# Chunks 8 and 9 transposed by the DMA crossbar, with shallower load buffers and a moved schedule, in a fused RetNet recurrence and gated FFN

## The chip, the cores and the metric

The kernel runs on one core of one Trainium2 chip. The metric is the device time of one execution in microseconds. Each run was repeated, and the times below are medians with all or the extreme runs beside them. In the profile, PE is TensorE, PEld its weight loads, DVE is VectorE, ACT is ScalarE, POOL is GpSimd and SP is SyncE. A "q" behind an engine's name (SPq) stands for its queue, from which DMAs are issued. "L183" is line 183 of the kernel that the profile belongs to. In the changed kernel the lines from L60 to about L530 carry a number one lower than in the kernel before.

With one core there is no other core to compare with, so a run is called slow when it is over 1.5% above the fastest run of the same kernel.

## The reference

The first part is a linear recurrence over 768 steps in 4 batches and 8 heads of width 64. Its output, as 3072 tokens of width 512, goes through a sigmoid-gated feed-forward of width 1536.

```python
state = gamma[None, :, None, None] * state + np.einsum('bhd,bhe->bhde', k[:, :, t], v[:, :, t])
y[:, :, t] = scale * np.einsum('bhd,bhde->bhe', q[:, :, t], state)
...
x = np.ascontiguousarray(attn_out.transpose(0, 2, 1, 3)).reshape(B * S, H * D)
gate = 1.0 / (1.0 + np.exp(-(x @ w_gate)))
val = x @ w_val
return (gate * val @ w_out).astype(np.float32)
```

## The kernel before

The recurrence is done in 24 chunks of 128 tokens, six for each batch. A chunk needs its k and q transposed. Then come the scores (k times q), masks on VectorE, the product of the masked scores with v, and the sum of k times v that is handed on as the state. The feed-forward runs over six blocks t of 512 tokens, that is four chunks each. The work of later chunks is put between the matmul groups of block t, according to a plan of (group number, step, chunks).

There are two ways to transpose. Chunks 4 to 9 use TensorE, with a copy by ScalarE behind it. Chunks 10 to 23 use the DMA crossbar, issued by SyncE. The loads are issued by GpSimd.

```python
ld = ctx.enter_context(tc.tile_pool(name="ld", bufs=10))
...
def load_v(g):
    vf[g] = ld.tile([C, H, D], F32, tag="vf", name="vf", bufs=8)
    nc.gpsimd.dma_start(out=vf[g], in_=src(v, g))

def load_kq(g):
    kn[g] = ld.tile([C, H, D], BF16, tag="kn", name="kn")      # 10 buffers
    qn[g] = ld.tile([C, H, D], BF16, tag="qn", name="qn")
    nc.gpsimd.dma_start(out=kn[g], in_=src(k, g))
    nc.gpsimd.dma_start(out=qn[g], in_=src(q, g))
...
def transposes(g):                                             # on TensorE
    tp = bank([128, 2 * NP, C], BF16)
    for i, x in enumerate((kn[g], qn[g])):
        for p in range(NP):
            nc.tensor.transpose(tp[:, i * NP + p, :], pair(x, p), ident)
    qkT[g] = at.tile([128, 2 * NP, C], BF16, tag="qkT", name="qkT", bufs=6)
    nc.scalar.activation(qkT[g], tp, AX.Copy)

def xbar(g):                                                   # by the DMA crossbar
    qkT[g] = ld.tile([128, 2 * NP, C], BF16, tag="qkX", name="qkX", bufs=8)
    for i, x in enumerate((kn[g], qn[g])):
        nc.sync.dma_start_transpose(out=qkT[g][:, i * NP:(i + 1) * NP, :],
                                    in_=x.rearrange("s h d -> s (h d)"))
...
def block(done, new):   # two chunks' outputs and the next two chunks' scores
    for g in olds: inter(g)
    for g in news: scores(g)
    for g in olds: intra(g)
    if news:
        zz[new] = pz.tile([128, 2, NP, D], F32, tag="z", name="z")
        for i, g in enumerate(news):
            if g % NCH < NCH - 1:      # a batch's last chunk hands no state on
                state(g, zz[new][:, i], True)
    ...                                # (cut: y_out, masks, state sums)
...
1: [(0, casts, 6), (1, step_t, 9), (3, block, 6, 8), (5, casts, 8), (7, scale_v, 10), ...
```

`step_t` is the TensorE transpose with the scaling of v; `scale_v` is that scaling alone. At t = 1 the first ups are split in halves of 256 columns, so that they can start on the first half of the tokens.

Of the kernel before, what the change touches and what calls it, by code (L numbers as in the profile page):

```python
# [9 lines left out]
F32 = mybir.dt.float32  # L10
# [7 lines left out]
def kernel(  # L18
# [11 lines left out]
    B, H, S, D = q.shape  # L30
    N_TOK, D_MODEL = out.shape
    D_FF = moe_w_gate.shape[1]
    C = 128
# [7 lines left out]
    ctx.enter_context(tc.manual_schedule())  # L41
    const = ctx.enter_context(tc.tile_pool(name="const", bufs=1))
    wpool = ctx.enter_context(tc.tile_pool(name="wpool", bufs=1))
    ld = ctx.enter_context(tc.tile_pool(name="ld", bufs=10))
    at = ctx.enter_context(tc.tile_pool(name="at", bufs=2))
    ffn = ctx.enter_context(tc.tile_pool(name="ffn", bufs=3))
    pz = ctx.enter_context(tc.tile_pool(name="pz", bufs=1, space=bass.MemoryType.PSUM))
# [2 lines left out]

    NG = B * NCH
    NT = N_TOK // 512
    XBAR = 10
    qn, kn, vf = {}, {}, {}

    def src(x, g):
        b, c = divmod(g, NCH)
        return x[b, :, c * C:(c + 1) * C, :].rearrange("h s d -> s h d")

    def load_v(g):  # L60
        vf[g] = ld.tile([C, H, D], F32, tag="vf", name="vf", bufs=8)
        nc.gpsimd.dma_start(out=vf[g], in_=src(v, g))  # L62

    def load_kq(g):
# [5 lines left out]
    def load_chunk(g):  # L70
        load_kq(g)
        load_v(g)
# [80 lines left out]
    def bank(shape, dt=F32):  # L153
        return pf.tile(shape, dt, tag="ff", name="ff")
# [12 lines left out]
    def xbar(g):  # L167
# [4 lines that stand above are left out]
# [68 lines left out]
    def x_cols(t, kk, lo, hi):  # L240
        if hi - lo == 512:
            return xT[t][:, :, kk, :]
        half = lo // 256
        return xT[t][:, half, kk, lo - half * 256:hi - half * 256]
# [132 lines left out]
    def up(t, n1, lo=0, hi=512):  # L377
        if t not in hT:
            hT[t] = ffn.tile([128, NFF, 512], BF16, tag="hT", name="hT", bufs=2)
        ps = []  # L380
        for w in (wg, wv):
            u = bank([128, 512])
            for kk in range(KT):
                nc.tensor.matmul(u[:, lo:hi], w[:, kk, n1 * 128:(n1 + 1) * 128], x_cols(t, kk, lo, hi),  # L384
                                 start=(kk == 0), stop=(kk == KT - 1))
            ps.append(u)
        gs = ffn.tile([128, 512], F32, tag="gs", name="gs")
        nc.scalar.activation(gs[:, lo:hi], ps[0][:, lo:hi], AX.Sigmoid)  # L388
        nc.vector.tensor_tensor(hT[t][:, n1, lo:hi], gs[:, lo:hi], ps[1][:, lo:hi], op=ALU.mult)  # L389

    def up_columns(t, n1s, lo, hi, rows=1):
        if t not in hT:
            hT[t] = ffn.tile([128, NFF, 512], BF16, tag="hT", name="hT", bufs=2)
        n = hi - lo
        us = [bank([128, 512]), bank([128, 512])]
        for row in range(rows):
            for w, u in zip((wg, wv), us):
                for i, n1 in enumerate(n1s):
                    for kk in range(row * KT // rows, (row + 1) * KT // rows):
                        nc.tensor.matmul(u[:, i * n:(i + 1) * n], w[:, kk, n1 * 128:(n1 + 1) * 128],  # L400
                                         x_cols(t, kk, lo, hi), start=(kk == 0 and (rows == 1 or i == 0)),
                                         stop=(kk == KT - 1), skip_group_check=rows > 1)
        ps = [u[:, :len(n1s) * n] for u in us]
        gs = ffn.tile([128, 512], F32, tag="gs", name="gs")
        g = gs[:, :len(n1s) * n]
        nc.scalar.activation(g, ps[0], AX.Sigmoid)  # L406
        nc.vector.tensor_tensor(hT[t][:, n1s[0]:n1s[-1] + 1, lo:hi], g.rearrange("p (i n) -> p i n", n=n),  # L407
                                ps[1].rearrange("p (i n) -> p i n", n=n), op=ALU.mult)
# [22 lines left out]
    def last_down(t):  # L431
        row = t * 512 + 384
        first = 0
        for i, width in enumerate((256, 128, 128)):
            o = bank([128, 512])
            for n1 in range(NFF):
                nc.tensor.matmul(o[:, :width], hT[t][:, n1, 384:512], wo[:, n1, first:first + width],  # L437
                                 start=(n1 == 0), stop=(n1 == NFF - 1))
            ob = ffn.tile([128, width], F32, tag=f"ob{width}", name="ob", bufs=2)
            if i == 1:  # L440
                nc.scalar.copy(ob, o[:, :width])
                nc.scalar.dma_start(out=out[row:row + 128, first:first + width], in_=ob)
            else:
                nc.vector.tensor_copy(ob, o[:, :width])
                nc.sync.dma_start(out=out[row:row + 128, first:first + width], in_=ob)
            first += width
# [78 lines left out]
    def ups(t):  # L525
        return [lambda n1=n1: up(t, n1) for n1 in range(NFF)]

    def downs(t):
        return [lambda sm=sm, i=i: down(t, sm, i) for sm in range(4) for i in range(2)]

    plan = {
        0: [(6, step_t, 4), (7, step_t, 5), (8, block, None, 4), (9, step_t, 6), (10, casts, 4), (10, step_t, 7),
            (12, block, 4, 6), (13, step_t, 8)],
        1: [(0, casts, 6), (1, step_t, 9), (3, block, 6, 8), (5, casts, 8), (7, scale_v, 10), (9, scale_v, 11),
            (11, block, 8, 10), (13, casts, 10), (14, scale_v, 12), (15, scale_v, 13), (18, block, 10, 12),
            (20, casts, 12)],
        2: [(0, scale_v, 14), (1, scale_v, 15), (4, block, 12, 14), (6, casts, 14), (11, scale_v, 16),
            (12, scale_v, 17), (16, block, 14, 16), (18, casts, 16)],
        3: [(3, scale_v, 18), (4, scale_v, 19), (6, block, 16, 18), (8, casts, 18), (12, scale_v, 20),
            (13, scale_v, 21), (15, block, 18, 20), (17, casts, 20)],  # L540
        4: [(3, scale_v, 22), (4, scale_v, 23), (6, block, 20, 22), (8, casts, 22), (14, block, 22, None)],
        5: [],
    }
    for t in range(NT):
        groups = ups(t) + downs(t)
        if t == NT - 1:
            groups[-2:] = [lambda: last_down(t)]
        if t == 0:
            groups = groups[6:]
            for g in range(8, 12):  # L550
                load_chunk(g)
        if t == 1:
            groups[:6] = [lambda n1=n1: up(1, n1, 0, 256) for n1 in range(6)]
            groups[6:6] = [lambda n1=n1: up_columns(1, range(n1, n1 + 2), 256, 512) for n1 in range(0, 6, 2)]
            for g in range(12, 16):
                load_chunk(g)
        if t == 2:
            load_chunk(18)
            load_chunk(19)
        if t == 3:  # L560
            load_chunk(22)
            load_chunk(23)
        for i, group in enumerate(groups):
            if t == 1 and i == 0:
                for g in range(XBAR, 12):
                    xbar(g)
            if i == len(groups) - 9:
                for g in range(4 * t + 8, 4 * t + 12):
                    if 12 <= g < NG:
                        xbar(g)  # L570
            if t == 1 and i == len(groups) - 4:
                load_chunk(16)
                load_chunk(17)
            if t == 2 and i == len(groups) - 4:
                load_chunk(20)
                load_chunk(21)
            group()
            for at_group, step, *g in plan[t]:
                if at_group == i:
                    step(*g)  # L580
# [30 lines left out]
```

## Time and profile before

| | before |
|---|---|
| median of 3 runs | 232.27 us (232.14 to 233.26) |
| span of the profiled run | 229.6 us |
| TensorE busy | 222.0 us, 97% of the span |
| DMA row full (9 tenths or more) | from the second to the 21st of 40 slices, to about 121 us; 7 tenths in the 22nd |
| granted clock | 1.00 |
| loads of k, q and v, median from issue to landing | 11.1, 12.4 and 10.5 us |

TensorE sets the end, so a microsecond saved or lost there is one in the time, as long as its inputs are there.

### The profile page before, as it was taken

Reading aid. Unit: us, or ns where it says so; the run is one execution under the profiler, and the core shown is the slowest. Engines: PE = TensorE matmul, PEld = TensorE weight load, DVE = VectorE, ACT = ScalarE, POOL = GpSimd, SP = SyncE. Lnnn points to the kernel's source line nnn. Section 1 sums busy time; section 2 is a strip of 40 time slices with the busy share of each in tenths; the row PEclk is TensorE's granted clock in tenths of the full one; section 3 lists DMA queues with packets and bytes.
Section 4 is the critical chain, followed back from the end, with each engine's and each line's share of the span. In section 5 each row is a group of like instructions: output and inputs, shape, how many; then the busy total and the mean of one; then the engine's idle time right before and its main releaser. Section 6 shows DMA issues by size and latency. Waiting matters only on the chain.

```text
span 229.6 us, 4530 instructions
## 1 busy us (share of the span) xinstructions
PE 222.0 (97%) x1834; PEld 120.9 (53%) x1834; DVE 119.1 (52%) x226; ACT 88.1 (38%) x161; POOL 75.3 (33%) x98
## 2 busy tenths in 40 slices
PE   4989999999999999999999999999999999999994
PEld 1558844558785455454445445445445454444444
DVE  5679444449875927458336267637267621243301
ACT  5964332465452423426321532612532512433221
POOL 7998666997843346723300000000000000000000
PEclk9999999999999999999999999999999999999999
DMA  7999999999999999999997342011100012100022
GB/s 140 179 228 197 198 206 207 235 241 246 178 155 108 158 147 175 251 123 135 121 177 190 104 91 46 0 50 64 74 3 0 0 49 91 46 0 3 0 91 93
DMA packets 75477, 27.56 MB, mean 120 GB/s; under 512 B 62016, under 2 KB 71104, under 8 KB 75456
## 3 DMA queue, kind: packets, MB, share of 16 engines
q0 software_dynamic: 55440, 16.78, 68.6%
q1 hardware_dynamic: 19872, 10.43, 24.5%
q8 instruction: 14, 0.23, 0.4%
q10 hardware_dynamic: 144, 0.07, 0.1%
q14 instruction: 7, 0.06, 0.1%
HBM read 28.31 MB, written 6.29 MB: 151 GB/s over the span
## 4 chain that ended last, share of the span: by engine, by line
PE 90%; POOL 3%; DMA 3%; ACT 1%; issue 1%; DVE 0%; POOLq 0%; ACTq 0%
PE ff L384 47%; PE ff L418 26%; PE ff L400 6%; DMA qr<-in_q_dram 3%; PE ff L233 2%; PE ff L184 2%; PE ff L196 2%; PE ff L163 1%; PE ff L437 1%; PE z L202 1%; POOL kr L77 1%; ACT gs L388 0%; POOL qr L77 0%; POOL vr L77 0%; POOL maskr L455 0%
## 5 line engine op out<-in xcount | busy, mean ns | idle before, releaser
L389 DVE TENSOR_TENSOR hT<-gs,ff 128x512 bf16<-128x512 f32 (+1 forms) x66 | 43.2, 662 | 58.9 <-PE ff L384 55.5
L384 PE MATMUL ff<-xT,wg 128*128 128x512 bf16 (+1 forms) x264 | 65.2, 369 | 0.0
L384 PE MATMUL ff<-xT,wv 128*128 128x512 bf16 (+1 forms) x264 | 65.2, 369 | 0.0
L388 ACT ACTIVATE gs<-ff 128x512 f32<-128x512 f32 (+1 forms) x66 | 38.0, 578 | 67.4 <-PE ff L384 61.4
L418 PE MATMUL ff<-wo,hT 128*128 128x512 bf16 x276 | 62.2, 379 | 0.0
L418 PEld LDWEIGHTS <-hT 128*128 128x128 bf16 x276 | 26.3, 98 | 30.5
L384 PEld LDWEIGHTS <-wv 128*128 128x128 bf16 x264 | 25.8, 98 | 28.6
L384 PEld LDWEIGHTS <-wg 128*128 128x128 bf16 x264 | 25.3, 98 | 27.5
L423 ACT COPY ob<-ff 128x512 f32<-128x512 f32 x23 | 13.5, 585 | 49.6 <-PE ff L418 49.4
L251 DVE TENSOR_TENSOR xT<-ff,taby 128x512 bf16<-128x512 f32 x20 | 12.9, 686 | 24.7 <-PE ff L233 24.7
L62 POOL DMA_DIRECT2D vf<-in_v_dram x20 | 18.0, 900 | 17.8 <-DMA qn<-in_q_dram 6.1
L67 POOL DMA_DIRECT2D kn<-in_k_dram x20 | 17.8, 890 | 17.1 <-PE ff L384 6.3
L68 POOL DMA_DIRECT2D qn<-in_q_dram x20 | 17.9, 893 | 2.6 <-DMA wo<-in_moe_w_out_dram 1.6
L208 ACT CAST zbd<-za 64x256 bf16<-64x256 f32 x38 | 15.3, 403 | 7.0 <-DVE za L220 4.8
L175 DVE TENSOR_TENSOR vs<-vf,tabv 128x512 bf16<-128x512 f32 x20 | 13.4, 686 | 2.1 <-DMA vf<-in_v_dram 2.1
L190 DVE TENSOR_TENSOR stB<-ff,causal 128x512 bf16<-128x512 f32 x20 | 13.6, 682 | 0.0
L189 DVE TENSOR_TENSOR stA<-ff,causal 128x512 bf16<-128x512 f32 x20 | 13.6, 682 | 0.0
L400 PE MATMUL ff<-xT,wg 128*128 128x256 bf16 x72 | 9.5, 273 | 0.3 <-DVE xT L342 0.3
L400 PE MATMUL ff<-xT,wv 128*128 128x256 bf16 x72 | 9.5, 273 | 0.0
L429 PE MATMUL ff<-ident 128*128 128x512 bf16 x18 | 6.3, 487 | 3.0 <-POOL ident masks.py:199 3.0
L407 DVE TENSOR_TENSOR hT<-gs,ff 128x512 bf16<-128x512 f32 x9 | 6.1, 684 | 5.0 <-PE ff L400 3.7
L406 ACT ACTIVATE gs<-ff 128x512 f32<-128x512 f32 x9 | 5.2, 596 | 6.5 <-PE ff L400 6.5
(84 smaller groups left out, 154.8 us busy)
## 6 DMA issues: line engine op xcount, KB each, us to landing
out_dram<-ob SPq DMA_DIRECT2D x23, 256.0 KB, 2.2
vf<-in_v_dram POOLq DMA_DIRECT2D x20, 256.0 KB, 10.5
kn<-in_k_dram POOLq DMA_DIRECT2D x20, 128.0 KB, 11.1
qn<-in_q_dram POOLq DMA_DIRECT2D x20, 128.0 KB, 12.4
wg<-in_moe_w_gate_dram POOLq DMA_DIRECT2D x6, 256.0 KB, 8.1
wv<-in_moe_w_val_dram POOLq DMA_DIRECT2D x6, 256.0 KB, 8.7
wo<-in_moe_w_out_dram POOLq DMA_DIRECT2D x4, 384.0 KB, 11.4
vr<-in_v_dram SPq DMA_DIRECT2D x1, 512.0 KB, 4.2
```

Of the source, the lines that this page charges most:

```text
L62: nc.gpsimd.dma_start(out=vf[g], in_=src(v, g))
L67: nc.gpsimd.dma_start(out=kn[g], in_=src(k, g))
L68: nc.gpsimd.dma_start(out=qn[g], in_=src(q, g))
L189: nc.vector.tensor_tensor(stA[g], sc[g][0], causal4, op=ALU.mult)
L190: nc.vector.tensor_tensor(stB[g], sc[g][1], causal4, op=ALU.mult)
L208: nc.scalar.copy(zbd[g % 4][half, :, half], z[half])
L384: nc.tensor.matmul(u[:, lo:hi], w[:, kk, n1 * 128:(n1 + 1) * 128], x_cols(t, kk, lo, hi), start=(kk == 0), stop=(kk == KT - 1))
L388: nc.scalar.activation(gs[:, lo:hi], ps[0][:, lo:hi], AX.Sigmoid)
L389: nc.vector.tensor_tensor(hT[t][:, n1, lo:hi], gs[:, lo:hi], ps[1][:, lo:hi], op=ALU.mult)
L400: nc.tensor.matmul(u[:, i * n:(i + 1) * n], w[:, kk, n1 * 128:(n1 + 1) * 128], x_cols(t, kk, lo, hi), start=(kk == 0 and (rows == 1 or i = ...
L418: nc.tensor.matmul(o, hT[t][:, n1, sm * 128:(sm + 1) * 128], wo[:, n1, :], start=(n1 == 0), stop=(n1 == NFF - 1))
L423: nc.scalar.copy(ob, o)
```

## The change

The change means to take the last transposes that stand beside the dense part of block t = 1 off TensorE. To make room on the DMA engines it lets the k, q and v loads run at most four chunks ahead, so that the loads of chunks 12 and on queue behind the crossbar transposes. The blocks of t = 1 are moved back in the plan, and ten ups instead of six are split in halves.

```diff
-    ld = ctx.enter_context(tc.tile_pool(name="ld", bufs=10))
+    ld = ctx.enter_context(tc.tile_pool(name="ld", bufs=4))
-        vf[g] = ld.tile([C, H, D], F32, tag="vf", name="vf", bufs=8)
+        vf[g] = ld.tile([C, H, D], F32, tag="vf", name="vf", bufs=6)
@@ plan
-            (12, block, 4, 6), (13, step_t, 8)],
-        1: [(0, casts, 6), (1, step_t, 9), (3, block, 6, 8), (5, casts, 8), (7, scale_v, 10), (9, scale_v, 11),
-            (11, block, 8, 10), (13, casts, 10), (14, scale_v, 12), (15, scale_v, 13), (18, block, 10, 12),
-            (20, casts, 12)],
-        2: [(0, scale_v, 14), (1, scale_v, 15), (4, block, 12, 14), (6, casts, 14), (11, scale_v, 16),
+            (12, block, 4, 6), (13, scale_v, 8)],
+        1: [(0, casts, 6), (2, scale_v, 9), (7, block, 6, 8), (9, casts, 8), (10, scale_v, 10), (11, scale_v, 11),
+            (12, block, 8, 10), (14, casts, 10), (16, scale_v, 12), (17, scale_v, 13), (19, block, 10, 12),
+            (21, casts, 12)],
+        2: [(0, scale_v, 14), (1, scale_v, 15), (6, block, 12, 14), (8, casts, 14), (11, scale_v, 16),
@@ the crossbar transposes, by (t, group)
+    xbars = {(0, 12): [8], (1, 0): [9, 10, 11, 12, 13], (2, 0): [14, 15],
+             (2, 11): [16, 17, 18, 19], (3, 11): [20, 21, 22, 23]}
@@ at t == 1
-            groups[:6] = [lambda n1=n1: up(1, n1, 0, 256) for n1 in range(6)]
-            groups[6:6] = [lambda n1=n1: up_columns(1, range(n1, n1 + 2), 256, 512) for n1 in range(0, 6, 2)]
+            groups[:10] = [lambda n1=n1: up(1, n1, 0, 256) for n1 in range(10)]
+            groups[10:10] = [lambda n1=n1: up_columns(1, range(n1, n1 + 2), 256, 512) for n1 in range(0, 10, 2)]
@@ ... (cut: the old placing of xbar(g) at t == 1 and at len(groups) - 9, replaced by xbars)
```

## The prediction

> **What bounds the kernel now.** I read the page first, then the chain that ended last in order of time, then the timeline of the SyncE queue with the landing times of the transposes.
>
> ```profile
> PE 222.0 (97%) x1834; PEld 120.9 (53%) x1834; DVE 119.1 (52%) x226; ACT 88.1 (38%) x161; POOL 75.3 (33%) x98
> DMA  7999999999999999999997342011100012100022
> PE 90%; POOL 3%; DMA 3%; ACT 1%; issue 1%; DVE 0%; POOLq 0%; ACTq 0%
> ```
>
> PE is busy for 97% of the span and is 90% of the chain; the DMA row is full from the second slice to the 22nd, that is until about 126 us (each slice is 229.6/40 = 5.74 us). So PE sets the time, and the DMA engines are the second resource: in that stretch they are never idle, and whatever is added to them lands later. The chain after 21 us is nothing but PE, with one exception:
>
> ```profile
> 53.60 0.45 PE ff L163 x8
> 54.05 1.75 PE ff L384 x16
> 55.80 0.45 PE ff L163 x8
> 56.24 0.45 PE ff L384 x4
> ...
> 56.73 0.40 ACT zbd L208
> 57.13 0.01 issue
> 57.15 0.41 ACT zbd L208
> 57.56 0.02 issue
> 57.57 0.38 ACT gs L388
> 57.96 0.50 ACT qkT L165
> 58.46 0.30 issue
> 58.76 0.68 ACT gs L388 x2
> 59.43 0.04 issue
> 59.48 0.38 PE ff L184 x7
> ```
>
> L163 with 8 instructions is the PE transpose of one chunk; the two shown are chunks 8 and 9, 0.45 us each. Between 56.70 and 59.48 the chain leaves PE for ScalarE: PE waits for PSUM banks that late sigmoids free, and for the copy of chunk 9's transposes (L165). In these 2.78 us PE does the rest of the third half-width up (0.44), the fourth (0.87), the eight L196 of the block (0.45) and 9 of 16 L184 (0.31): 2.07 us. It loses 0.7 us.
>
> ```profile
> 55.34 1.38 SPq L170 DMA_TRANSPOSE qkX<-kn  x1
> 56.77 2.48 SPq L170 DMA_TRANSPOSE qkX<-qn  x1
> 59.29 1.28 SPq L170 DMA_TRANSPOSE qkX<-kn  x1
> 60.69 1.24 SPq L170 DMA_TRANSPOSE qkX<-qn  x1
> ...
> 83.25 10.03 SPq L425 DMA_DIRECT2D out_dram<-ob  x4
> ```
>
> These are the crossbar transposes of chunks 10 and 11. Narrowing the view of L170 to one of them at a time gives issue to landing of 8.3, 9.4, 9.5 and 11.5 us, so they land at 63.6, 66.1, 68.8 and 72.2. The eight of 128 to 140 us, when no load is on its way, take 2.4 us in the median and follow each other every 1.31 us. Chunk 11 lands at 72.2; its scores (L184) start at 73.5 in the chain. So the kernel before has only 1.3 us to spare at that point.
>
> **What the Trainium skill says.** "TensorE: Matmul & The Clock Gate", section "Wait — 56ns, not 53.3ns?", gives back-to-back matmuls N ÷ 2.4 GHz plus about 2.5 ns. The trace agrees: 8 transposes in 0.45 us are 56 ns each, 40 L384 in 8.63 us are 216 ns. "DMA: Bandwidth & Descriptors", section "Queues, rings and completion order", says that an engine goes round-robin between queue rows with work, packet by packet. The trace fits that: an output store lands 2.0 us after its issue late in the kernel and after 6.1 us at 42 us, with loads queued. The same page, section "DMA Transpose (X-bar)", has plain DMA transposes issued from Sync or Scalar only; here all 28 stand on SyncE, in order with the stores, so one that waits holds the stores behind it.
>
> **The change part by part.** (1) Removed: PE transposes of chunks 8 and 9, 2 x 0.45 = 0.90 us, all of it on the chain. Two ScalarE copies of 1.03 us go with them, and two PSUM banks.
>
> (2) The wait of 0.7 us. Its L165 part (chunk 9's copy) is gone. The casts (four L208, 1.66 us, from 55.89) remain and still hold back the second sigmoid until 57.57. Six half-width ups now have to find banks while VectorE still works off the masks until 56.3. Working the seven banks through in order of release, the fifth half-width up waits about 0.15 us for the first product and 0.25 us more for the second sigmoid. So 0.4 us stays, 0.3 us is won.
>
> (3) Four more ups are split in halves: 32 matmuls of 216 ns become 64 of 109 ns (48 L400 in 5.24 us): 64 x 109 - 32 x 216 = 0.07 us lost.
>
> Sum on PE, if nothing arrives late: 0.90 + 0.30 - 0.07 = 1.1 us won.
>
> (4) Added: four transposes, 4 x 1.31 = 5.2 us of DMA time in the stretch that is full already. (5) Taken from that stretch: with 4 buffers in place of 10, the load of k for chunk 12 waits for the state matmuls of chunk 8, at about 62.5 us; before, loads of chunks 12 and 13 were issued from 53.2. That defers six loads; loads alone land 0.81 us apart (chunks 4 to 7 in the landing times), 4.9 us in all. So the two nearly cancel by the time chunk 11 is wanted. Chunk 8's own load now waits for chunk 4's state matmuls (43.96 to 44.2 us in the chain) instead of being issued at 41.8; but that load took 7.2 us to land because others were ahead of it, so it should land near 49 us as before, and chunk 10's (after 52 us) near 55.5.
>
> When do the transposes land against when PE wants them? My unit costs come from 53 to 91.3 us of the kernel before: 23 loads x 0.81, 12 transposes x 1.31 and stores of 1.2 make 35.5 us in 38.3 us, so 93% efficiency: 0.87 us a load and 1.41 us a transpose when mixed. By 53 us in the new kernel chunk 8 and the k and q of chunk 9 are there.
> - Chunk 9: PE starts t=1 at 53.6 and has 8 half-ups x 0.874 = 7.0 plus 0.4 of waits, so the block begins at 61.0 and wants it after L196 (0.45) and eight L184 (0.27): 61.7. DMA: four transposes 5.6, about two loads between them 1.7, stores 1.2: 61.5. Even.
> - Chunk 11: PE: block to 62.8, seven groups of 7.0 us, plus 0.72: 70.5. DMA from 53: eight transposes 11.3, six loads 5.2, stores 1.2, one load of chunk 12 mixed in: 71.7. Late by 1.2 us.
> - Chunk 13: PE: 83.2 plus the 1.2 of before = 84.4. DMA: twelve transposes 16.9, 14 loads 12.2, stores 1.2: 83.3. In time.
> - Chunks 14, 15: issued after the last store of t=1 (about 92), wanted at about 103; at most 8 us. Later chunks have more room (chunks 22 and 23 load at about 140 us, wanted at 173).
>
> So of 1.1 us about 0.7 to 1.2 us is given back: I put the gain at 0.4 us, 231.9 us.
>
> **Rivals.** First, everything arrives in time: 1.1 us or, with the bank wait gone too, 1.5 us faster, 230.8 to 231.2. For it: the depth limit was plainly chosen to clear the way for these transfers, and loads stop competing at 57 to 62 us. Against it: 1.3 us of slack before, and the block of chunks 8 to 11 is wanted one full-width up earlier (eight instead of nine before it). Second, the transposes run late as those of before did, with 8 to 11 us each: chunk 9 lands at 65 to 66 instead of 61.7, PE stands for 3 to 4 us and, as loads are now gated by PE's progress, part of that repeats at the next block: 234 to 236. For it: the latencies shown. Against it: those had a queue of loads behind them without end, these have two chunks. Third, loads gated by four buffers starve PE later: against it stands 5 us and more of room per block after 92 us. It would add 1 to 3 us.
>
> **Range and chances.** PE's work is known to 0.1 us, so the best possible is about 230.6 (both 0.9 and 0.7 won). The transposes' landing I know to about 2 us, and only lateness costs: hence 230.5 to 234.0. 2% is 4.6 us: faster than 227.6 has no source in the profile; slower than 236.9 needs the second rival in full with the gap repeated. Faster 0.01, same 0.95, slower 0.04.
>
> **What would show it.** Right: 32 L163 instead of 48 and 0.90 us less of them in the chain; no L165 in the chain near 58 us; a wait of PE at L184 of chunks 10 and 11 near 70 us that ends on a transpose, of about 1 us. Step 2 is wrong if the casts no longer appear in the chain, or if the wait at 57 us keeps its 0.7 us. Step 5 is wrong if chunk 8 is loaded much after 49 us, or if the transposes of chunks 8 and 9 take over 8 us; then the wait sits at the first block near 62 us and the time is above 233. If PE waits nowhere after 58 us the first rival holds.

## The result, and the profile after

The changed kernel took 235.68 us in the median of four runs (235.51, 263.47, 235.84, 234.62), the kernel before 232.22 us on the same chip (232.14 to 233.26). The run of 263.47 had a granted clock of 0.855 and is left out as slow. The ratio of the fast runs is 1.0123, with a 95% interval of 1.0074 to 1.0172. Ratios here are the mean time of one kernel's fast runs over that of the other's in the same rounds, so they are not quite the ratio of the medians. By the 2% rule the class is "same". Both median and interval say that the change loses 3 us or so, and the prediction of 231.9 us with its range up to 234.0 was wrong.

First the page of the kernel after: busy time by engine, then the rows of 40 slices with the granted clock and the DMA engines, then the chain's shares by engine.

```profile
PE 222.7 (95%) x1850; PEld 124.1 (53%) x1850; DVE 119.0 (51%) x228; ACT 86.8 (37%) x161; POOL 75.4 (32%) x98
...
PEclk9999999999979999999999999999999999999998
DMA  8999999999989936976992930992200011100022
...
PE 90%; DMA 6%; ACT 1%; SPq 1%; issue 1%; DVE 0%; POOLq 0%
```

The engine that bounds the kernel has lost 2 points of its share, and the chain's DMA share has doubled. The clock row has one slice of 7 tenths, the 12th, which runs from 64.3 to 70.1 us (slices of 233.8/40 = 5.85 us). The 8 in the last slice comes after TensorE's last matmul, at 230.6 us, and costs nothing. The DMA row has gaps from the 15th slice on, so the smaller buffers did thin out the traffic. The median load of k now lands 5.6 us after its issue instead of 11.1.

The chain of work that ended last, in order of time (start, us, what), shows what happens in that slice:

```profile
57.35 7.90 DMA qkX<-qn
65.25 0.14 issue
65.38 0.61 PE ff L183 x8
65.99 0.99 PE ff L232 x16
66.98 0.43 PE z L201 x16
67.41 2.54 PE ff L383 x16
```

TensorE stands for the crossbar transpose of chunk 9's q: issued at 57.35, landed at 65.25, then the eight score matmuls of chunk 9 at L183. The list of TensorE's waits gives this as one wait of 3.2 us, and the timeline as 3.17. The next three lines are slow as well. In a kernel that does not wait here (the keep_warm experiment below) the 16 L232 take 0.57 and the 16 L201 0.25 us.

SyncE's queue (start, us of issuing, instruction) shows how chunk 9 came to be so late. The first two lines are chunk 8's k and q, the last two chunk 9's:

```profile
50.56 1.33 SPq L169 DMA_TRANSPOSE qkX<-kn  x1
51.94 1.25 SPq L169 DMA_TRANSPOSE qkX<-qn  x1
54.70 0.34 SPq L424 DMA_DIRECT2D out_dram<-ob  x1
55.09 2.14 SPq L169 DMA_TRANSPOSE qkX<-kn  x1
57.35 1.44 SPq L169 DMA_TRANSPOSE qkX<-qn  x1
```

Narrowed to single instructions, the view gives their landing. Chunk 8's two land after 3.7 and 2.8 us, at 54.25 and 54.70. Chunk 9's land after 7.5 and 7.9 us, at 62.59 and 65.25. In the meantime GpSimd's queue (start, us of issuing, instruction, idle time before it and what ended it) issued six loads, k, q and v of chunks 10 and 11, from the first line here to the second:

```profile
52.83 0.89 POOL L66 DMA_DIRECT2D kn<-in_k_dram  x1 [4.91 <-PE z L201]
...
57.18 0.93 POOL L61 DMA_DIRECT2D vf<-in_v_dram  x1
67.03 0.88 POOL L66 DMA_DIRECT2D kn<-in_k_dram  x1 [8.92 <-DMA qkX<-kn]
```

These six land at 56.57, 58.72, 60.64, 61.83, 63.67 and 64.91. All of them are down before chunk 9's q. The third line is the load of k for chunk 12. It waits for a transpose: the k of chunk 11, which lands at 66.47. The view of the DMA engines from 60 to 62 us (packets, MB, and the time of the packets as a share of 16 engines; over 100% means that packets were under way side by side) puts the loads (q0) beside the transposes (q1). Three of these were issued and not yet landed at 60 us (chunk 9's two and chunk 10's k), five by 62 us:

```profile
q0 software_dynamic: 1926, 0.35, 245.3%
q1 hardware_dynamic: 95, 0.02, 8.3%
```

The same view of 64 to 66 us, when the loads are done:

```profile
q1 hardware_dynamic: 1727, 0.42, 125.8%
q0 software_dynamic: 1, 0.00, 0.0%
```

With loads beside them the transposes got 95 packets in 2 us; without, 1727, and the four transposes of chunks 10 and 11 are then down within a few microseconds, by 66.9. So the transposes stood back as long as loads were on their way.

The slow lines after the wait have their own cause. The windows (us, busy time and count by engine, then granted clock, DMA share and GB/s) show it to a fifth of a microsecond:

```profile
65.40:65.60 0.20, 0.20 (x6) 0.20 (x8) 0.00 (x0) 0.00 (x0) 0.00 (x0) 0.50 1.29 294
68.60:68.80 0.20, 0.20 (x2) 0.15 (x1) 0.20 (x1) 0.20 (x1) 0.20 (x2) 0.53 0.27 17
68.80:69.00 0.20, 0.20 (x4) 0.18 (x2) 0.20 (x2) 0.00 (x0) 0.20 (x1) 1.00 0.89 58
```

The clock is at half speed from about 65.4 to 68.8, that is for 3.4 us, in which 1.7 us of work is lost. It begins at the end of the wait. The Trainium skill, page "TensorE: Matmul & The Clock Gate", section "What's actually happening", describes a free-running window of 3413 ns that halves the clock after an idle window. This trace agrees with the 3.4 us and the 0.50. The wait before it may be shorter than that window: 3.17 us here, 3.03 us in early9_b5 (half speed from 65.8 to 69.2 us) and 2.58 us in later_block (from 67.7 to 71.1 us). The length of the wait alone doesn't decide: when the changed kernel was run again, its profiled run waited 3.30 us at the same place and kept a clock of 1.00. A free-running window would explain that; no run here tests it. The nine fast executions of the changed kernel split the same way: 234.62 and 234.98 us at a clock of 0.999 and 1.0, and seven of 235.39 to 237.21 (mean 236.05) at 0.983 to 0.993.

The profiled runs of before and after (231.38 and 235.51 us; spans 229.6 and 233.8) can be balanced. Block t = 1 starts its ups at 53.89 in both, although the kernel after has 0.45 us of chunk 8's transposes less in front of it; so its start-up ran 0.45 us later. It did so before the schedules part: the first long run of half-ups (64 matmuls, L400 or L399) starts at 21.18 us before and 21.62 after, and at 21.3 to 21.7 in pe89, depth4_before and keep_warm below. The wait is 3.17, the clock about 1.7. That is 5.3 us, the span grew by 4.2, so 1.1 us was won. This is good to a few tenths only: counted to the end of TensorE's last matmul (226.7 and 230.6 us) the growth is 3.9, and 1.4 us are left.

### The profile page after: what moved, and what is told of

Read it like the earlier page. It is cut to its first block, busy times and chain, and to the rows that moved or that the text cites. A ratio compares the mean times of both kernels' runs of the same rounds, so it can differ in the third digit from the quotient of the medians.

```text
span 233.8 us, 4589 instructions
## 1 busy us (share of the span) xinstructions
PE 222.7 (95%) x1850; PEld 124.1 (53%) x1850; DVE 119.0 (51%) x228; ACT 86.8 (37%) x161; POOL 75.4 (32%) x98
## 4 chain that ended last, share of the span: by engine, by line
PE 90%; DMA 6%; ACT 1%; SPq 1%; issue 1%; DVE 0%; POOLq 0%
PE ff L383 43%; PE ff L417 26%; PE ff L399 8%; DMA qkX<-qn 3%; PE ff L232 3%; DMA kr<-in_k_dram 2%; PE ff L183 2%; PE ff L195 2%; PE ff L436 1%; PE ff L263 1%; PE z L201 1%; SPq L169 1%; PE ff L162 1%; PE ff L287 1%; PE ff L312 1%
## 5 line engine op out<-in xcount | busy, mean ns | idle before, releaser
L388 DVE TENSOR_TENSOR hT<-gs,ff 128x512 bf16<-128x512 f32 (+1 forms) x66 | 42.1, 646 | 59.9 <-PE ff L383 54.6
L383 PE MATMUL ff<-xT,wg 128*128 128x512 bf16 (+1 forms) x264 | 64.0, 365 | 0.2 <-DVE hT L388 0.2
L383 PE MATMUL ff<-xT,wv 128*128 128x512 bf16 (+1 forms) x264 | 63.8, 364 | 0.1
L387 ACT ACTIVATE gs<-ff 128x512 f32<-128x512 f32 (+1 forms) x66 | 37.0, 565 | 67.3 <-PE ff L383 64.2
L383 PEld LDWEIGHTS <-wg 128*128 128x128 bf16 x264 | 25.6, 98 | 26.6 <-issue 0.4
L61 POOL DMA_DIRECT2D vf<-in_v_dram x20 | 18.5, 925 | 1.5 <-DMA wo<-in_moe_w_out_dram 1.1
L399 PE MATMUL ff<-xT,wg 128*128 128x256 bf16 x88 | 11.6, 273 | 0.3 <-DVE xT L341 0.3
L399 PE MATMUL ff<-xT,wv 128*128 128x256 bf16 x88 | 11.6, 273 | 0.0
L405 ACT ACTIVATE gs<-ff 128x512 f32<-128x512 f32 x11 | 6.5, 597 | 11.5 <-PE ff L399 8.6
L406 DVE TENSOR_TENSOR hT<-gs,ff 128x512 bf16<-128x512 f32 x11 | 7.4, 684 | 5.4 <-PE ff L399 3.7
L399 PEld LDWEIGHTS <-wg 128*128 128x128 bf16 x88 | 8.4, 98 | 1.7 <-issue 0.6
```

Source lines behind the costliest of these rows:

```text
L383: nc.tensor.matmul(u[:, lo:hi], w[:, kk, n1 * 128:(n1 + 1) * 128], x_cols(t, kk, lo, hi), start=(kk == 0), stop=(kk == KT - 1))
L387: nc.scalar.activation(gs[:, lo:hi], ps[0][:, lo:hi], AX.Sigmoid)
L388: nc.vector.tensor_tensor(hT[t][:, n1, lo:hi], gs[:, lo:hi], ps[1][:, lo:hi], op=ALU.mult)
L399: nc.tensor.matmul(u[:, i * n:(i + 1) * n], w[:, kk, n1 * 128:(n1 + 1) * 128], x_cols(t, kk, lo, hi), start=(kk == 0 and (rows == 1 or i = ...
```

## The experiments

Sixteen runs were made, two of them repeats, in four batches, each beside the kernel before (medians 231.87, 232.0, 232.12 and 231.88 us, eleven runs each). All gave the right result. Where no other base is named, a diff is against the changed kernel. Runs marked s are "slow" by the 1.5% rule. Their clock of 0.972 to 0.993 is one to four half-speed stretches as above (estimate: 1.7 us of 234 is 0.007). In the five that were profiled these follow waits; for the others that is likely, not shown. The ratio drops them, which flatters kernels with a wide spread. The expectations were often right on the landing and too low on the time: early9, hold_loads, hold11, depth10 and pe89_depth10 came out 3 to 8 us above the highest time expected of them.

| kernel | median us | ratio to before, fast runs (95%) | longest waits of TensorE for a crossbar transpose |
|---|---|---|---|
| after_again | 235.88 | 1.0176 (1.0147 to 1.0205) | 3.30, chunk 9 |
| depth10 | 245.92 | 1.0499 (1.0449 to 1.0548) | 6.25, chunk 9; 5.33, chunk 15 |
| depth4_before | 231.57 | 0.9981 (0.9955 to 1.0007) | none |
| pe89 | 231.0 | 0.996 (0.9948 to 0.9971) | none |
| pe89_again | 231.46 | 0.9998 (0.9965 to 1.0031) | none |
| pe89_depth10 | 236.77 | 1.0099 (1.0038 to 1.016) | 1.79, chunk 15 |
| pe9 | 231.95 | 0.9992 (0.9962 to 1.0022) | none |
| pe89_spare | 234.57 | 1.0082 (1.004 to 1.0125) | 3.63, chunk 13 |
| keep_warm | 234.73 | 1.012 (1.009 to 1.015) | hidden by filler matmuls |
| early9 | 235.58 | 1.0032 (1.0002 to 1.0061) | 1.07, chunk 9; 1.72, chunk 13 |
| later_block | 234.28 | 1.004 (0.9995 to 1.0086) | 2.58, chunk 9 |
| later_early9 | 236.75 | 1.0215 (1.0175 to 1.0254) | 1.99, chunk 13 |
| hold_loads | 241.32 | 1.0382 (1.0346 to 1.0418) | 3.74, chunk 10; 5.99, chunk 11 |
| hold11 | 239.65 | 1.0321 (1.0279 to 1.0363) | 4.41, chunk 13 |
| early9_gate8 | 235.8 | 1.0056 (1.0029 to 1.0083) | 1.25, chunk 11 |
| early9_b5 | 234.34 | 1.0033 (1.0005 to 1.006) | 3.03, chunk 9 |

The theory was: chunk 9's transposes are late because the loads of chunks 10 and 11 go ahead of them; the wait costs some 3 us and the clock some 1.7 more. The rivals were that the schedule or the buffers cost the time, and that the four added transposes overload this stretch wherever they are put.

### The parts of the change alone

**pe89: the new schedule and buffers, but chunks 8 and 9 transposed by TensorE as before.**

```diff
-            (12, block, 4, 6), (13, scale_v, 8)],
-        1: [(0, casts, 6), (2, scale_v, 9), ...
+            (12, block, 4, 6), (13, step_t, 8)],
+        1: [(0, casts, 6), (2, step_t, 9), ...
-    xbars = {(0, 12): [8], (1, 0): [9, 10, 11, 12, 13], (2, 0): [14, 15],
+    xbars = {(1, 0): [10, 11, 12, 13], (2, 0): [14, 15],
```

> The changed kernel with chunks 8 and 9 transposed by PE again (new schedule of blocks and new depth alone). If the late transposes are all of the loss: no wait over 0.5 us in this stretch, 0.9 us of transposes back, 231.9 to 232.5 us. If the new depth or the moved blocks cost time themselves (chunks 10 to 13 late): over 233 us, with a wait at the blocks near 70 or 83 us.

Measured: 231.0 us (230.84 to 231.16), and TensorE waits for no crossbar transpose. So the loss is in the four added transposes, and the schedule and the buffers don't cost anything. (The time is below the 231.9 to 232.5 us that I expected.) As this was the fastest kernel of all, it was run once more.

**pe89_again: the same kernel, five rounds.**

> The version with both chunks on PE once more, on this chip beside the changed kernel: 230.8 to 231.3 us, 0.3 to 0.5% faster than before, no wait of PE after 58 us, small spread.

Measured: 231.46 us (230.95 to 231.88, one run of 233.54 at a clock of 0.991) against 231.88. The chain of that run, where the changed kernel has its wait:

```profile
62.16 0.22 PE ff L195 x4
62.39 0.55 PE ff L183 x16
```

All 16 score matmuls of chunks 8 and 9 run in one go. The gain over the kernel before is 0.4% in the first batch and within the interval in the second, so I call it 0 to 0.5%, and not certain.

**depth10: the change with the old buffers (10, and 8 for v).**

```diff
-    ld = ctx.enter_context(tc.tile_pool(name="ld", bufs=4))
+    ld = ctx.enter_context(tc.tile_pool(name="ld", bufs=10))
-        vf[g] = ld.tile([C, H, D], F32, tag="vf", name="vf", bufs=6)
+        vf[g] = ld.tile([C, H, D], F32, tag="vf", name="vf", bufs=8)
```

> The changed kernel with the load buffers of the kernel before (10 of k and q, 8 of v). Theory M: more loads run beside the transposes of chunks 8 and 9, as beside those of the kernel before (8.3 to 11.5 us each): chunk 9's q lands at 64 to 69 us, the wait for it is 3 to 7 us, 235.5 to 239 us. Rival D (it is the smaller depth that made the transposes late, by loading chunks 8, 10 and 11 later): wait gone, under 232 us.

Measured: 242.12, 244.91, 246.92s and 247.36s us. Chunk 9 lands at 65.61 and 68.42, 10.4 and 11.7 us after issue. The timeline line of its scores (start, us, instruction, wait before it and what ended it):

```profile
68.56 0.61 PE L183 MATMUL ff<-qkX 64*128 64x128 bf16 x8 [6.25 <-DMA qkX<-qn]
```

More loads beside the transposes make them later. The smaller buffers are what saves the change from 10 us more of loss.

**depth4_before: the kernel before, with the new buffers alone.** The diff, against the kernel before, is that of depth10 read backwards.

> The kernel before with the smaller load depth alone (4 of k and q, 6 of v). If the depth is what made the version with both on PE 0.9 us faster than before: 230.8 to 231.3 us. If it was the later block with its removed wait of 0.7 us: 231.6 to 232.2 us, equal to before; the transposes of chunks 10 and 11 land several us earlier than 66.1 and 72.2 either way.

Measured: 231.57 us (231.49 to 232.15), 0.9981 with an interval that includes 1. Chunk 11's last transpose lands at 64.52 instead of 72.2, so the smaller buffers bring it 7.7 us earlier, room that the old kernel doesn't need: it had no wait there.

**pe89_depth10: pe89 with the old buffers.** Both diffs above together.

> Chunks 8 and 9 on PE, new places of the blocks, but the load depth of the kernel before. If the smaller depth is needed by the new schedule (transposes of chunks 10 and 11 land at 66 and 72 us with the old one, wanted at 71): a wait of about 1 us, 231.5 to 232.5 us. If the new schedule alone made the gain: 231.0 us or less.

Measured: 232.98, 235.97, 240.02s, 238.0s, 236.71s and 236.83s us. So the new schedule needs the smaller buffers. The reason is not the one that I expected, a wait for chunk 11 near 71 us: in the profiled run, which was the fastest, chunk 11 lands at 70.35, before its scores at 71.12. TensorE waits for chunk 15, whose q lands at 106.30 (in pe89 at 99.41):

```profile
106.44 0.40 PE L183 MATMUL ff<-qkX 64*128 64x128 bf16 x8 [1.79 <-DMA qkX<-qn]
```

Where the five slower runs wait is not known.

**pe9: chunk 8 by the crossbar, chunk 9 by TensorE.** The diff is that part of pe89 which concerns chunk 9.

> The changed kernel with chunk 9 alone transposed by PE; chunk 8 stays with the crossbar. Theory M (late because loads run beside it): chunk 8's transposes run at 50.5 to 54.7 us, where only the tail of chunk 9's loads is on its way, and land seven us before they are wanted; one PE transpose (0.45 us) less than with both on PE, no wait of PE: 230.4 to 230.8 us, the fastest so far (both on PE: 231.0). If any crossbar transpose at this place disturbs the loads of chunks 10 and 11, those and their transposes land late and it is over 231.3 us.

Measured: 231.95 us (231.33 to 232.37), no wait for a transpose. My expectation of 230.4 to 230.8 was missed: taking 0.45 us of transposes off TensorE brought nothing measurable over pe89 (231.0 and 231.46 us, in other batches). Why is open.

**pe89_spare: pe89, with the crossbar transposes of chunks 8 and 9 issued all the same, into tiles that nobody reads.**

```diff
     def xbar(g):
-        qkT[g] = ld.tile([128, 2 * NP, C], BF16, tag="qkX", name="qkX", bufs=8)
+        to = ld.tile([128, 2 * NP, C], BF16, tag="qkX", name="qkX", bufs=8)
+        if g > 9:
+            qkT[g] = to
         for i, x in enumerate((kn[g], qn[g])):
-            nc.sync.dma_start_transpose(out=qkT[g][:, i * NP:(i + 1) * NP, :],
+            nc.sync.dma_start_transpose(out=to[:, i * NP:(i + 1) * NP, :],
                                         in_=x.rearrange("s h d -> s (h d)"))
```

The other hunks are those of pe89, except that `xbars` stays as in the changed kernel.

> Chunks 8 and 9 transposed by PE, and the four crossbar transposes of chunks 8 and 9 issued all the same, where the change has them, into tiles that nobody reads. It separates traffic from dependency. If only the wait for chunk 9 costs time (the DMA engines have room for the rest): within 0.4 us of both on PE, 230.8 to 231.4 us. If the added traffic itself makes chunks 10 to 13 late: 232 us or more, with a wait at the scores near 70 or 83 us.

Measured: 239.42s, 232.41, 235.34, 233.51, 234.28 and 234.87 us. No one waits for chunk 9 here, yet the five fast runs are at 1.0082 of the kernel before, and those of pe89 at 0.996: 1.2%, or 2.8 us. Of the fast runs there is no profile. In the profiled run, the one of 239.42, which is slow, the wait has moved to chunk 13 (the scores are L185 in this kernel):

```profile
89.47 0.61 PE L185 MATMUL ff<-qkX 64*128 64x128 bf16 x8 [3.63 <-DMA qkX<-qn]
```

That is the last of the rivals above: the four transposes cost time even where nobody waits for them. Whether it is their traffic, their place ahead of the others in SyncE's queue or the buffers of k and q that they keep in use, this run doesn't separate: chunk 11's k lands at 69.71 here, at 63.74 in pe89.

**after_again: the changed kernel, five rounds.**

> The changed kernel unaltered, to have its spread from as many runs as the others: 234.5 to 236 us, some runs above, by how long PE waits for chunk 9 and whether the clock drops.

Measured: 234.98 to 237.21 us, median 235.88, all classed fast; ratio 1.0176 (class "unclear" by the 2% rule, as the interval goes to 1.0205, but clear of 1). The wait sits at chunk 9 again (3.30 us, landed at 65.90). The loss is confirmed in a batch of its own.

### The clock

**keep_warm: fourteen matmuls without use before the scores of chunk 9, so that TensorE does not stand idle.**

```diff
         for g in news:
+            if g == 9:
+                keep_on(14, pz.tile([128, 4, 128], F32, tag="z", name="z"))
             scores(g)
```

> The changed kernel with 14 idle matmuls of 512 columns (14 x 0.216 = 3.0 us) on PE between the scores of chunk 8 and of chunk 9, that is inside the wait of 3.2 us. If the low clock after the wait (0.63 from 65.4 to 70.0 us in the profiled run, so about 1.7 us lost there) is a part of the loss: the clock stays 1.00, the work after the wait takes its usual time, 233.5 to 234.5 us with less spread than 234.6 to 235.8. If the low clock costs nothing that matters: 235 to 236 us.

Measured: 234.44 to 235.75 us, median 234.73, all six at a clock of 1.00. The chain (start, us, what):

```profile
62.32 3.13 PE z L430 x14
65.45 0.04 issue
65.50 0.40 PE ff L183 x8
65.89 0.57 PE ff L232 x16
```

The filler ends at 65.45, and chunk 9 landed at 65.36, so hardly anything is lost to it; and the work behind runs at full speed. So the half-speed clock is a consequence of the idle time. Its share of the loss is the 1.15 us between the medians of keep_warm and after_again, though the two were in different batches and their ranges overlap; the wait itself is the rest.

### Moving chunk 9's transposes or its use

**early9: chunk 9's transposes issued together with chunk 8's.**

```diff
-    xbars = {(0, 12): [8], (1, 0): [9, 10, 11, 12, 13], (2, 0): [14, 15],
+    xbars = {(0, 12): [8, 9], (1, 0): [10, 11, 12, 13], (2, 0): [14, 15],
```

> The changed kernel with one edit: chunk 9's two crossbar transposes issued right behind chunk 8's, ahead of the fourth output store of the first token tile. Theory M (a transpose lands late when loads are queued beside it: chunk 9's, issued at 55.1 and 57.4 us, met the loads of chunks 10 and 11 issued from 52.8 us on): issued about 2 us earlier, at 53.2 and 54.5, chunk 9 still overlaps the loads, k lands at 55 to 58 and q at 57 to 61 instead of 65.3, before the scores want it at 62.2; no wait of PE there, clock stays 1.00, time 230.8 to 231.5 us. Theory U (my prediction's unit cost: each transpose takes 1.4 us of DMA time in the mix): chunk 9 by 61.5, chunk 11 late by about 1.2 us at the next block, 231.5 to 232.5 us.

Measured: 233.98, 238.43s, 238.93s, 237.17s, 231.93 and 233.41 us. The timeline of TensorE in the profiled run (233.98):

```profile
63.12 0.40 PE L183 MATMUL ff<-qkX 64*128 64x128 bf16 x8 [1.07 <-DMA qkX<-qn]
...
86.89 0.40 PE L183 MATMUL ff<-qkX 64*128 64x128 bf16 x8 [1.72 <-DMA qkX<-qn]
```

Issued at 53.10 and 54.41, chunk 9's transposes still take 7.2 and 8.6 us (landed at 60.28 and 62.99). The first wait shrinks from 3.17 to 1.07 us, but a second one appears at chunk 13, where the changed kernel has none. So an earlier issue cures a part of the first wait only, and pays for it later. The transpose of q had at most three loads ahead of it (issued at 52.67, 53.55 and 54.41) and still took 8.6 us; three more loads were issued behind it by 57.02.

**later_block: the blocks two half-ups later, all twelve ups split.**

```diff
-            (12, block, 8, 10), (14, casts, 10), (16, scale_v, 12), (17, scale_v, 13), (19, block, 10, 12),
+            (14, block, 8, 10), (16, casts, 10), (17, scale_v, 12), (18, scale_v, 13), (20, block, 10, 12),
@@ (cut: block 6, 8 from group 7 to 9, casts and scale_v with it, and range(10) to range(12))
```

> The changed kernel with all twelve ups of the second token tile split and the block of chunks 6 to 9 two half-ups (1.75 us) later. The transposes are not moved by PE's progress before that block, so chunk 9 still lands at about 65; the wait for it falls from 3.2 to about 1.5 us and the low clock with it; later chunks as before: 232.3 to 234 us. If traffic as a whole is the bound, the wait turns up again at chunk 11 or 13 and the time stays over 234.5 us.

Measured: 235.68s, 234.15, 231.5, 234.42, 236.05s and 232.4 us. In the profiled run (235.68) the scores come later, but chunk 9 lands later too, at 67.07, and TensorE waits 2.58 us for it:

```profile
67.20 0.40 PE L183 MATMUL ff<-qkX 64*128 64x128 bf16 x8 [2.58 <-DMA qkX<-qn]
```

The lowest run, 231.5, suggests that the wait can be absent; it was not profiled.

**later_early9: both edits together.**

> Both: chunk 9's transposes ahead of the store, and the block 1.75 us later. Chunk 9 at about 63 (as in the run with the early issue), wanted at 64: no wait there. If the wait for chunk 9 is all of the loss: 230.5 to 231.3 us. If the added traffic makes chunk 13 late as in the run with the spare transposes: 231.5 to 236 us with a large spread and the wait at chunk 13 near 86 us.

Measured: 233.28, 236.49, 237.08s, 239.12s, 237.0s and 236.11 us. No wait for chunk 9, which lands at 62.90; TensorE waits 1.99 us for chunk 13 at 86.19 even in the fastest run, the profiled one.

### Holding the loads back

**hold_loads: the loads of chunks 10 to 15 wait until chunk 9 is transposed**, by a tiny GpSimd copy that reads chunk 9's result ahead of them in the queue.

```diff
+    held = const.tile([128, 1, 1], BF16, name="held")
@@ in the loop over xbars
                 xbar(g)
+                if g == 9:
+                    nc.gpsimd.tensor_copy(held, qkT[9][:, NP:NP + 1, 0:1])
+                    for n in range(10, 16):
+                        load_chunk(n)
@@ (cut: their load_chunk calls at t == 0 and t == 1 go)
```

> The changed kernel with one edit: a tiny GpSimd copy that reads chunk 9's transposed q stands ahead of the loads of chunks 10 to 15, so no load is issued until chunk 9's transposes have landed; those stay where they are, behind the store. Theory M (loads beside it): they land 2.4 to 3.7 us after issue as chunk 8's did, by 60.5 us, no wait for chunk 9 at 62 us; chunks 10 and 11 then load from about 60 us, their transposes land at about 68 to 71, so a wait of 0 to 2 us may come at the next block (70.5): 231 to 233.5 us. Rival O (order: they stand behind the store and SyncE issues them slowly, whatever the loads do): they still land at 62.6 and 65.3, the wait of 3.2 us stays and another comes for chunk 11, 236 us or more.

Measured: 238.94 to 242.03 us and one of 244.43s. SyncE's queue in the profiled run (244.43, slow by the rule) for chunk 9's k and q:

```profile
55.96 2.13 SPq L169 DMA_TRANSPOSE qkX<-kn  x1
58.21 1.20 SPq L169 DMA_TRANSPOSE qkX<-qn  x1
```

They land at 59.59 and 60.65, after 3.6 and 2.4 us instead of 7.5 and 7.9, and nobody waits for chunk 9. That shows what held them up: the loads. The clock has no part in this, as the landing is one of DMAs and comes before the first wait. It costs more than it wins, as chunks 10 and 11 are loaded too late:

```profile
75.49 0.61 PE L183 MATMUL ff<-qkX 64*128 64x128 bf16 x8 [3.74 <-DMA qkX<-qn]
...
82.09 0.61 PE L183 MATMUL ff<-qkX 64*128 64x128 bf16 x8 [5.99 <-DMA qkX<-qn]
```

**hold11: the same, but only the loads of chunk 11 and on are held.** The diff is that of hold_loads with `range(11, 16)`, and chunk 10 loaded as in the changed kernel.

> The changed kernel; chunk 10 loads as in it, chunk 11 only after chunk 9's transposes have landed: half the dose of the experiment that held both. Theory L (loads issued beside the transposes pass ahead of them: in the changed kernel all six loads of chunks 10 and 11 landed before chunk 9's second transpose; alone a load takes 0.81 us): three loads fewer, chunk 9 lands about 2.5 us earlier, at 62 to 63 instead of 65.3, the wait for it is under 1 us, the clock stays up; chunk 11 then lands at 70 to 73 against 70.5 to 71.5 wanted, a wait of 0 to 2 us: 232 to 234.5 us. Theory P (the position in SyncE's order behind the store decides): chunk 9 lands at 65 as before, over 235 us.

Measured: 238.27 to 241.51 us, median 239.65. Chunk 9's q is issued at 58.04 and lands at 63.01, so it takes 4.97 us with three loads ahead of it, against 7.90 with six (the changed kernel) and 2.44 with none (hold_loads, issued at 58.21). The six cost 0.91 us each, the three 0.84: close to the 0.87 us a load of the prediction. This holds where all the loads were issued ahead; in early9, with three ahead and three close behind, it doesn't. TensorE doesn't wait for chunk 9. Chunk 11 is then transposed by 71.77 only, the load of k for chunk 12 is issued at 71.77, and chunk 13 comes too late:

```profile
89.84 0.61 PE L183 MATMUL ff<-qkX 64*128 64x128 bf16 x8 [4.41 <-DMA qkX<-qn]
```

### The gate of chunk 12's load

In every run with four buffers but hold_loads (and early9_gate8, which was built to avoid it) the load of k for chunk 12 goes out about 0.56 us after chunk 11's k transpose has landed: 66.47 and 67.03 in the changed kernel, 69.52 and 70.08 in early9, 63.74 and 64.30 in pe89, 68.31 and 68.87 in later_block. Chunk 11 is the last of its batch and hands no state on, so its k is free as soon as it is transposed, ahead of those of chunks 8 to 10, and the built program puts chunk 12's k into that buffer. So loads of 12 and 13, and then their transposes, hang on chunk 11's transpose. Two kernels tried to loosen this in early9.

**early9_gate8: early9, with chunk 11's k kept in use by a one-element copy after the block, so that chunk 12 takes chunk 8's buffer.**

```diff
+    keep = const.tile([128, 1, 1], BF16, name="keep")
+    def keep_k11():
+        nc.scalar.copy(keep, kn[11][:, 0:1, 0:1])
-            (12, block, 8, 10), (14, casts, 10), ...
+            (12, block, 8, 10), (12, keep_k11), (14, casts, 10), ...
@@ (cut: xbars as in early9)
```

> Chunk 9's transposes ahead of the store (as in the run early9), and a one-element ScalarE copy of chunk 11's k behind the block of chunks 8 to 11, so that the load of chunk 12's k no longer takes chunk 11's buffer (free only after chunk 11's transpose: issued at 70.1 us there) but chunk 8's (free after chunk 8's state matmuls, about 64 us). Theory G (that gate is what makes chunk 13 late once chunk 9 is in time): chunk 12 loads about 5 us earlier, chunk 13's transposes land by 83 instead of 86.9, no wait at chunk 13, 231 to 233 us. Theory T (the traffic itself is too much, loads then run beside the transposes of chunks 10 and 11): those land later, 72 to 76, a wait at chunk 11, over 234 us.

Measured: 233.16, 233.81, 232.66, 238.77s, 240.05s and 237.79s us. In the profiled run (233.16) the load of k for chunk 12 goes out at 64.41 instead of 70.08, and chunk 13 lands at 82.20 instead of 86.85, without a wait. So the gate was the cause at chunk 13. But now these loads run beside chunk 11's transposes, which land at 73.31, and the wait is there:

```profile
73.44 0.40 PE L183 MATMUL ff<-qkX 64*128 64x128 bf16 x8 [1.25 <-DMA qkX<-qn]
```

**early9_b5: early9 with five buffers for k and q.**

```diff
-        kn[g] = ld.tile([C, H, D], BF16, tag="kn", name="kn")
-        qn[g] = ld.tile([C, H, D], BF16, tag="qn", name="qn")
+        kn[g] = ld.tile([C, H, D], BF16, tag="kn", name="kn", bufs=5)
+        qn[g] = ld.tile([C, H, D], BF16, tag="qn", name="qn", bufs=5)
@@ (cut: xbars as in early9)
```

> early9 with five buffers of k and of q in place of four: chunk 12's k waits for chunk 7's state matmuls (about 52 us) and loads as soon as the queue of GpSimd gets to it, about 58 us; chunk 13's waits for chunk 11's transpose. Theory T: three more loads run beside the transposes of chunks 9 to 11, chunk 9 lands after 64, waits at chunk 9 and 11, over 235 us. Theory G: chunk 12 early, chunk 13 still behind the gate: about as early9 (231.9 to 238.9 us), no better.

Measured: 235.58s, 237.9s, 236.2s, 231.96, 232.95 and 233.1 us. In the profiled run (235.58, slow) chunk 9 lands at 61.80 and 65.25 and TensorE waits 3.03 us for it: the wait is back at chunk 9. No better than early9.

## Why the prediction was wrong, and what of it was right

**Steps 1 to 3, the work on TensorE: right in the main.** 32 matmuls of L162 instead of 48 are left, no copy of chunk 9 is in the chain near 58 us, and the block of chunks 6 and 8 began at 61.49 us with a start-up that was 0.45 late, against the predicted 61.0. Of the bank wait I predicted 0.4 us to stay; two gaps of about 0.35 and 0.26 us stayed, at 57.74 and 58.44, so 0.1 us was won there and not 0.3. The sum of 1.1 us won agrees with the 1.1 to 1.4 us that the balance of the two profiled runs leaves, but no experiment shows it: pe9, with one chunk off TensorE, was no faster than pe89.

**Step 5's first half, chunk 8: right on the time.** Its k and q were loaded by 49.2 us (predicted near 49) and its transposes took 3.7 and 2.8 us. The gate was another: the load went out at 42.63 us, after TensorE's transposes of chunk 5 (from 41.95), and not after chunk 4's state matmuls at 43.96. Chunk 5 is the last of its batch, like chunk 11 below.

**The step that failed is chunk 9: "four transposes 5.6, about two loads between them 1.7, stores 1.2: 61.5. Even."** That loads delay a transpose was right, and so was the cost of a load, 0.84 to 0.91 us. The term that was mis-sized is "about two loads". Six went ahead: every load of chunks 10 and 11, issued up to 57.18, landed before the q issued at 57.35. I had shared the engines out by a mean over a long stretch, and a transpose beside loads didn't get a mean share. hold11 (three loads) and hold_loads (none) show that it is the loads: the same transpose took 4.97 and 2.44 us there instead of 7.90.

With six loads the same sum is 5.6 + 5.2 + 1.2 = 12.0, from 53 us: 65.0, and 65.25 was measured. That it fits so well is in part luck, for its 1.41 us a transpose is not borne out. Once the loads were down, the four transposes of chunks 10 and 11 landed 0.42 to 0.48 us apart (65.53, 66.01, 66.47, 66.89). The 1.31 us that I had put down as "DMA time" is the pace at which SyncE issues them: the DMA share from 131 to 140 us in the kernel before was only 0.49. And the number of loads ahead is not the whole rule, as early9 shows.

**What followed was the second rival:** a landing at 65 to 66, TensorE standing for 3 to 4 us, 234 to 236 us. The landing, the wait of 3.17 us and the time of 235.68 are inside its figures. I had turned it down because "these have two chunks" of loads behind them only; two chunks are six loads, and six loads are 5 us. That rival had no place for the clock: 1.7 us more in most runs, shown by the 0.50 of the windows and by keep_warm's six runs at 1.00. The repeat at the next block that I had named did not come in the changed kernel, so that its total fits is in part luck too: the clock stands where the repeat was. It came in the experiments that removed the first wait.

**Step 5's gate was wrong as well.** I had the load of k for chunk 12 waiting "for the state matmuls of chunk 8, at about 62.5 us". It waits for the transpose of chunk 11, and went out at 67.03. It did not cause the wait in the changed kernel, which comes before; but it is why early9 waits at chunk 13, as early9_gate8 shows. For later_early9 and hold11, which wait there too, it is the likely reason.

**Chunk 11, "late by 1.2 us", did not happen.** Its transposes were reckoned for 71.7 us and landed at 66.9, ahead even of the 70.5 at which I had TensorE want them; its scores, held up by chunk 9, came after 75. The sum charged too much for a transpose. (Its own terms give 71.6. And the DMA row before is full to the 21st slice, 121 us, not to the 22nd; nothing rests on either.)

So 1.1 to 1.4 us was won, about 3.2 lost to one wait, and 1.7 to the clock where it dropped. Removing that wait alone doesn't give the gain back. In pe89_spare, where nobody needs the added transposes, the time is lost all the same, and each kernel that was freed of the wait for chunk 9 with its transposes still on the crossbar (hold_loads, hold11, later_early9, early9_gate8) waited for chunk 10, 11 or 13 in its profiled run. So in each of these kernels the added transposes cost time again. That the DMA engines lack the room for them is not shown: in the changed kernel the 15th and 16th slices of their row are at 3 and 6 tenths.

Two more things stay open. One is why the engines sometimes move so little when loads and transposes are mixed: early9 moved 62 GB/s from 58 to 60 us, the kernel before 215 in the same window. It may be the cause of the wide spread of early9 (231.93 to 238.93), but no run separates it. The other is whether pe89's gain is real.

## What to carry to other kernels

Before moving work from the bounding engine to a DMA queue, list what is under way beside the moved transfer, issued ahead of it or close behind, and let all of that land first, rather than giving it a mean share: here six loads stood in the way instead of two. Look for which buffer comes free first when buffers are few, as that decides what a later load waits for. And count a wait on TensorE of 2.6 us or more, as seen here, as possibly costing 1.7 us on top, for the clock that can drop behind it.

## What the Trainium skill lacked or had wrong

- "DMA: Bandwidth & Descriptors", section "Queues, rings and completion order", has each engine go round-robin between queue rows with work. In the kernel before that fits (272 load packets and 229 of SyncE's queue from 60 to 62 us). In the changed kernel the same 2 us had 1926 load packets and 95 of the transposes, with three to five transposes issued and not landed, of similar mean size (0.35 MB in 1926 and 0.02 MB in 95, some 200 bytes each). Chunk 9's q, issued behind six loads, landed after all of them; the page doesn't prepare for that, and no run here shows why.
- The same page, section "DMA Transpose (X-bar)", has no duration, and the page elsewhere only a bandwidth. (The page "VectorE: DVE Perf Modes", section "The three transpose paths", has 1309 ns for 128x128 in bf16, without a word on loads beside it.) Here one 128x512 bf16 transpose between two SBUF tiles mostly takes SyncE 1.2 to 1.3 us to issue (up to 3.4 in the kernel before). It lands after 2.4 us at the least, when no load is on its way, and beside loads after 7.5 and 7.9 us (chunk 9 in the changed kernel) or 8.3 to 11.5 us (chunks 10 and 11 in the kernel before).
- "TensorE: Matmul & The Clock Gate", section "What's actually happening", doesn't say how idle a window must be for the clock to halve. Here waits of 2.58, 3.03 and 3.17 us, all shorter than its 3.4 us, were followed by half speed, and one of 3.30 us and those up to 1.99 us (later_early9) were not.
